# Weight chunks asked for in another order, and the w_r groups of batch 1's first half moved into batch 0, in a three-stage transformer kernel on one core

## The chip, the cores and the metric

The kernel runs on one core of a Trainium2 chip. The metric is the device time of one execution in microseconds (us). The engines are TensorE (PE; its weight loads are shown as PEld), VectorE (DVE), ScalarE (ACT), GpSimd (POOL) and SyncE (SP). DMA requests here are issued on SyncE's and ScalarE's queues, and each queue works in order.

## The reference

Inputs are float32, but the products w_r, w_k and w_v arrive as 8-byte words (the raw tiles are int32 pairs) that the kernel converts itself. Eight batches of 576 tokens, 8 heads of 64:

```python
kv  = einsum('bhsd,bhse->bhde', k, v)          # per head, 64 x 64
out = einsum('bhsd,bhde->bhse', q, kv)
x   = out / sqrt(mean(out*out, -1) + 1e-6) * g_norm   # heads side by side: 512 columns
xp  = x shifted by one token
k2  = relu((mu_k*x + (1-mu_k)*xp) @ w_k) ** 2   # 512 -> 1024
v2  = k2 @ w_v                                  # 1024 -> 512
r   = sigmoid((mu_r*x + (1-mu_r)*xp) @ w_r)     # 512 -> 512
x2  = r * v2
# then a mixture of 4 experts, each a causal attention (two chosen per token); not touched by the change
```

## The kernel before

The program has two phases. Phase 1 makes x2 and writes it to memory, phase 2 (line 600 on) reads it and computes the experts. The change is in phase 1.

Every large product is done in three passes: both factors are split into a high part (rounded for the fast fp32 mode) and a low part, and `mm3` (L62 to L64) multiplies high by high, high by low and low by high into one accumulator. A batch is handled in two halves of 288 tokens. The steps are:

- `front(b)`: kv of all heads (L229, copied by ScalarE at L233), then for each half and pair of heads the product with q (L251), its square and its copy to xT (L256, L257), the mean of squares (L269), and the reciprocal root on VectorE (`rsqrt`, L276 to L291, 14 instructions, called "root" here; result rb). `scaled` spreads rb over the heads (TensorE, L299) and multiplies xT by it (VectorE, L302). For batch 0 each half has a root of its own, first and second root; the other batches have one.
- `mix(b, h, "r")` and `mix(b, h, "k")`: the token shift (xm, L354 and L355), its high part xh (L356) and its low part xl (L346 for batch 0's r mix, L348 else), for four blocks of 128 columns.
- `r_group` (four per half, w_r, sigmoid at L374), `k_group` (eight per half, w_k, L385 to L389), `v_group` (four per half, w_v, L401). Each is a chain of `mm3` into one of four accumulators named acc.

The weights come in 20 chunks of 512 KB: 4 of w_r, 8 of w_k, 8 of w_v, in this order. `wload` asks for a chunk on ScalarE's queue (L138, tile raw, three buffers). Its conversion begins with an Abs on ScalarE (L190, tile cvt), goes on with five steps on VectorE (L146, L148, L150, L155, L157) and a copy of the high part on ScalarE (L152), and ends with three matmuls that add up the low part (L183 to L185) and a copy (L186); for four chunks VectorE does the end (L179, L180). `wstep` issues one VectorE step, `wconv` finishes one chunk and opens the next; `wstep` stands between the steps of the root, and a table `TK` says after which pieces of batch 0's front a `wconv` stands. k, v and q are loaded on SyncE's queue. A DMA signals through one of eight semaphores that both queues share in turn, so that a request waits in its queue for the eighth DMA ahead of it, and holds what stands behind it there.

The order in which the code issues work is written by hand (generators that are advanced between groups). A scheduler then settles the order on each engine from what it takes to be ready; tiles of a pool wait for a free buffer.

Of the kernel before, what the change touches and what calls it, by code (L numbers as in the profile page):

```python
# [8 lines left out]
F32 = mybir.dt.float32  # L9
# [15 lines left out]
def tile_kernel(ctx: ExitStack, tc: tile.TileContext, qT, k, v, g2, mu_k, mu_r, w_r, w_k, w_v, w_qk, w_vg, w_o, out):  # L25
    nc = tc.nc
    P = 128
# [79 lines left out]
    def phase1():  # L107
        with ExitStack() as st1:
# [22 lines left out]

            VEC = (13, 15, 17, 19)

            def wload(i):
                if i < len(wts):
                    _, _, w, kt, c0 = wts[i]
                    raw = raws[i] = stg.tile([P, CW, 2], I32, name="raw", bufs=3)
                    nc.scalar.dma_start(raw.rearrange("p n t -> p (n t)"), w[kt * P:(kt + 1) * P, c0:c0 + CW].bitcast(I32))  # L138

            def words(i):  # L140
# [26 lines left out]
            def wconv():  # L167

                i = wat[0]
                wat[0] += 1  # L170
                if 0 < i <= len(wts):
                    for _ in ops.pop():
                        pass
                    wh, wl, _, kt, c0 = wts[i - 1]
                    x = cvs.pop(i - 1)
                    raws.pop(i - 1)
                    h, l = wh[:, kt, c0:c0 + CW], wl[:, kt, c0:c0 + CW]
                    if i - 1 in VEC:
                        nc.vector.tensor_sub(x, x, h.bitcast(F32))  # L179
                        nc.vector.tensor_add(l, x, l.bitcast(F32))  # L180
                    else:
                        acc = ps.tile([P, CW], F32, name="acc", bufs=4)
                        nc.tensor.matmul(acc, ident, x, start=True, stop=False)  # L183
                        nc.tensor.matmul(acc, idn, h, start=False, stop=False)
                        nc.tensor.matmul(acc, idn, l, start=False, stop=True)  # L185
                        nc.scalar.activation(l, acc, AF.Copy)  # L186
                    wload(i + 2)
                if i < len(wts):
                    t = cvs[i] = stg.tile([P, CW], F32, name="cvt", bufs=3)
                    nc.scalar.activation(t, raws[i][:, :, 1].bitcast(F32), AF.Abs)  # L190
                    ops.append(words(i))

# [24 lines left out]
            def front(b):  # L217
# [51 lines left out]
                                nc.tensor.matmul(sm[g:g + 32, :QS], sels[:, i, :], sqs[h, i // 2][:, i % 2, c * QS:(c + 1) * QS],  # L269
                                                 start=(i == 0), stop=(i == NP - 1), skip_group_check=True)  # L270

                def rsqrt(h0, h1):
                    g = slice(64 * h0, 64 * h1)
                    m, r, t, c = ms[g], y[g], nt[g], rb[g]

# [28 lines left out]
                if b == 0:  # L304

                    for h in range(2):
                        for a in range(2):
                            heads(h, a)
                            yield
                        means(h)  # L310
                        rsqrt(h, h + 1)
                        yield
                        scaled(h)
                        yield
                    return
                for h in range(2):
                    for a in range(2):
                        heads(h, a)
                    for _ in range(3):
                        yield  # L320
                means(0, 1)
                yield
                rsqrt(0, 2)
                for _ in range(5):
                    yield
                for h in range(2):
                    scaled(h)
# [37 lines left out]

            def r_group(b, h, m):
                if m == 0:
                    sgs[b, h] = sb.tile([P, KD, HS], F32, name="sg", bufs=2)
                sg = sgs[b, h]
                xh, xl = mixed[b, h, "r"]  # L370
                acc = ps.tile([P, HS], F32, name="acc", bufs=4)
                ms_ = slice(m * P, (m + 1) * P)
                mm3(acc, lambda i: wrh[:, i, ms_], lambda i: wrl[:, i, ms_], lambda i: xh[:, i, :], lambda i: xl[:, i, :], KD)
                nc.scalar.activation(sg[:, m, :], acc, AF.Sigmoid)  # L374
# [36 lines left out]
            sk = sb.tile([P, NP, S + 1], F32, name="xT").rearrange("p k t -> p (k t)")  # L411

            sk2 = [sb.tile([P, KF, HS], F32, name=name, bufs=1).rearrange("p k t -> p (k t)") for name in ("kh", "kl")]
            sq_ = sb.tile([P, KD, HS], F32, name="sg", bufs=2)
            for c in "w0 w1 w2 k0 k1 k2 k3 k4 q0 q1 q2 q3".split():
                i = int(c[1])
                if c[0] == "w":
                    wload(i)
                elif c[0] == "k":
                    load_kv(i, [sk[:, j * DM:(j + 1) * DM] for j in (2 * i - 6, 2 * i - 5)] if i > 2 else None)  # L420
                else:
                    load_q(i, sq_[:, :2, :] if i > 2 else None)
            for i in (3, 4):
                load_kv(NF + i, [t[:, (i - 3) * DM:(i - 2) * DM] for t in sk2])
            nc.sync.dma_start(g_sb, g2)
            nc.sync.dma_start(muk, mu_k)
            nc.sync.dma_start(mur, mu_r)
# [22 lines left out]
                for _ in range(n):  # L450
                    wconv()

            TK = [1, 0, 1, 1, 0, 1, 1, 1, 1, 1, 1]
            wconv()
            for i in range(7):
                run(f0)
                ticks(TK[i])
            mr = mix(0, 0, "r")
            for i in range(4):
# [16 lines left out]
            for b in range(B):  # L476
# [7 lines left out]
                for h in range(2):  # L484
                    nb, nh = (b, 1) if h == 0 else (b + 1, 0)
                    if b == B - 1 and h == 0:
                        stf.close()
                        weights2()
                    if b > 0:
                        for m in range(1, KD):  # L490
                            r_group(b, h, m)
                            run(f)
                    mr = mix(nb, nh, "r") if 0 < nb < B else None
                    for m in range(KF):
                        k_group(b, h, m)
                        run(f)
                        if b == h == 0:
                            wconv()
                        if m > 0:
                            run(mr)  # L500
                    if mr is not None:

# [374 lines left out]
```

## Time and profile before

| | us |
|---|---|
| median of 3 runs | 1022.28 |
| lowest and highest of them | 1021.43 and 1023.65 |
| profiled execution | 1020.85 |
| its span | 1018.8 |
| TensorE busy in the span | 987.1 (97%) |
| VectorE, ScalarE, GpSimd busy | 546.8, 500.2, 248.5 |

TensorE is busy for 97% of the span, and in the page's slices its first one shows 6 tenths and the next 7 and 8, all others 9 or more. The granted clock (PEclk) is 9 or 10 tenths in every slice but the second and third, 7 and 8 tenths. A row of a timeline gives the start, the length, the engine, the line, and in brackets how long the engine was idle before it and what ended that.

### The profile page before, as it was taken

The numbers are of one execution on the slowest core, as the hardware profiler recorded it, in microseconds if no ns is written. First come the engines' busy times: TensorE is split into PE (matmuls) and PEld (weight loads), VectorE is DVE, ScalarE is ACT, GpSimd is POOL, SyncE is SP. The second block draws the span as 40 slices with busy tenths as digits, with TensorE's granted clock in tenths as the row PEclk, the third lists the DMA queues.
The fourth block names the chain that finished last, engine by engine and source line by source line (L and its number), as shares of the span: only waits on it lengthen the run. The fifth ranks groups of instructions, "written<-read, shape, count | busy, mean of one in ns | idle before, by whom it ended". The sixth has DMA issues, their size and how long they took to land.

```text
span 1018.8 us, 21026 instructions
## 1 busy us (share of the span) xinstructions
PE 987.1 (97%) x8168; PEld 899.7 (88%) x8168; DVE 546.8 (54%) x1572; ACT 500.2 (49%) x1326; POOL 248.5 (24%) x408
## 2 busy tenths in 40 slices
PE   6789999999999999999999999999999999999998
PEld 3358999999999999999999999988989898888986
DVE  4889625535535535445355531476575655656552
ACT  4677426434533553463364533456463645464544
POOL 0001212102201210220131113265161625334321
PEclk9789999999999999999999999999999999999999
DMA  9572213041050050050002201211120202020102
GB/s 324 171 231 64 67 60 106 24 112 53 25 151 27 10 164 24 1 165 24 24 2 71 60 5 43 69 48 31 65 71 24 94 1 94 18 77 27 48 12 82
DMA packets 42034, 70.56 MB, mean 69 GB/s; under 512 B 3792, under 2 KB 21712, under 8 KB 41936
## 3 DMA queue, kind: packets, MB, share of 16 engines
q1 hardware_dynamic: 30608, 49.31, 15.4%
q10 hardware_dynamic: 11328, 19.93, 6.3%
q8 instruction: 64, 1.05, 0.5%
q14 instruction: 34, 0.28, 0.1%
HBM read 50.34 MB, written 18.87 MB: 68 GB/s over the span
## 4 chain that ended last, share of the span: by engine, by line
PE 80%; DMA 7%; ACT 4%; POOL 3%; DVE 3%; issue 1%; ACTq 0%; SPq 0%; DVEq 0%; POOLq 0%
PE acc L62 22%; PE acc L64 21%; PE acc L63 21%; PE acc L725 3%; PE pt L698 3%; DMA x2in<-x2d 3%; PE s L649 2%; PE po L251 2%; POOL pr L678 2%; POOL x2l L535 2%; ACT pr L661 2%; PE acc L229 1%; PE acc L269 1%; ACT x2h L534 1%; PE po L299 1%
## 5 line engine op out<-in xcount | busy, mean ns | idle before, releaser
L388 POOL TENSOR_TENSOR ksq<-rl 128x288 f32<-128x288 f32 x128 | 92.8, 727 | 502.8 <-ACT rl L385 475.8
L62 PE MATMUL acc<-xh,wkh 128*128 128x288 f32 x512 | 153.2, 299 | 0.0
L64 PE MATMUL acc<-xh,wkl 128*128 128x288 f32 x512 | 151.6, 296 | 0.0
L64 PE MATMUL acc<-kh,wvl 128*128 128x288 f32 x512 | 151.1, 296 | 0.0
L62 PE MATMUL acc<-kh,wvh 128*128 128x288 f32 x512 | 149.4, 297 | 0.5 <-ACT kh L386 0.4
L63 PE MATMUL acc<-kl,wvh 128*128 128x288 f32 x512 | 149.6, 293 | 0.2 <-DVE kl L389 0.2
L63 PE MATMUL acc<-xl,wkh 128*128 128x288 f32 x512 | 149.4, 292 | 0.0
L661 ACT ACTIVATE pr<-pr,nm 128x256 f32<-128x256 f32 (+4 forms) x144 | 83.2, 580 | 66.5 <-DVE nm L615 65.6
L389 DVE TENSOR_TENSOR kl<-ksq,kh 128x288 fp32r<-128x288 f32 x128 | 64.4, 507 | 72.3 <-POOL ksq L388 70.6
L62 PEld LDWEIGHTS acc<-xh,wkh 128*128 128x128 f32 x512 | 96.2, 188 | 7.1 <-issue 5.3
L678 POOL TENSOR_SCALAR pr<-pr,rc,wg 128x512 f32<-128x512 f32 (+3 forms) x128 | 76.6, 613 | 99.3 <-DVE wg L608 53.9
L63 PEld LDWEIGHTS acc<-kl,wvh 128*128 128x128 f32 x512 | 97.3, 190 | 0.7 <-DVE kl L389 0.4
L63 PEld LDWEIGHTS acc<-xl,wkh 128*128 128x128 f32 x512 | 97.4, 190 | 0.1
L62 PEld LDWEIGHTS acc<-kh,wvh 128*128 128x128 f32 x512 | 95.3, 188 | 1.4 <-ACT kh L386 0.9
L64 PEld LDWEIGHTS acc<-kh,wvl 128*128 128x128 f32 x512 | 96.1, 188 | 0.0
L64 PEld LDWEIGHTS acc<-xh,wkl 128*128 128x128 f32 x512 | 96.0, 188 | 0.0
L374 ACT ACTIVATE sg<-acc 128x288 f32<-128x288 f32 x64 | 25.9, 408 | 142.6 <-PE acc L64 142.6
L348 DVE TENSOR_TENSOR xl<-xm,xh 128x288 fp32r<-128x288 f32 x120 | 54.4, 487 | 75.9 <-ACT xh L356 75.3
L401 DVE TENSOR_TENSOR sg<-acc,sg 128x288 f32<-128x288 f32 x64 | 29.2, 457 | 105.9 <-PE acc L64 105.1
L385 ACT ACTIVATE rl<-acc 128x288 f32<-128x288 f32 x128 | 52.1, 414 | 58.7 <-PE acc L64 58.3
L62 PE MATMUL acc<-x2h,wqh 128*128 128x256 f32 (+1 forms) x256 | 78.6, 308 | 0.0
L62 PE MATMUL acc<-xh,wrh 128*128 128x288 f32 x256 | 77.1, 302 | 1.1 <-ACT wvl L186 1.1
(166 smaller groups left out, 2437.3 us busy)
## 6 DMA issues: line engine op xcount, KB each, us to landing
x2d<-sg SPq DMA_DIRECT2D x16, 576.0 KB, 3.3
qt<-in_qT SPq DMA_DIRECT2D x31, 288.0 KB, 4.8
out<-ob SPq DMA_DIRECT2D x28, 288.0 KB, 2.1
kt<-in_k SPq DMA_DIRECT2D x24, 256.0 KB, 5.2
vt<-in_v SPq DMA_DIRECT2D x24, 256.0 KB, 5.7
x2in<-x2d ACTq DMA_DIRECT2D x8, 640.0 KB, 4.4
raw<-in_w_k ACTq DMA_DIRECT2D x8, 512.0 KB, 4.5
raw<-in_w_v ACTq DMA_DIRECT2D x8, 512.0 KB, 3.5
```

The lines of the kernel that those rows point to most:

```text
L62: nc.tensor.matmul(ps, wh(i), xh(i), start=(i == 0), stop=False)
L63: nc.tensor.matmul(ps, wh(i), xl(i), start=False, stop=False)
L64: nc.tensor.matmul(ps, wl(i), xh(i), start=False, stop=(i == n - 1))
L348: nc.vector.tensor_sub(xl[:, p, :], xp, xh[:, p, :].bitcast(F32))
L385: nc.scalar.activation(rl, acc, AF.Relu)
L388: nc.gpsimd.tensor_mul(sq, rl, rl)
L389: late.append(lambda: nc.vector.tensor_sub(kl[:, m, :], sq, kh[:, m, :].bitcast(F32)))
L401: nc.vector.tensor_mul(sg[:, m, :], acc, sg[:, m, :])
L661: nc.scalar.activation(pr[:, :L], pr[:, :L], AF.Exp, bias=nm, scale=-1.0, accum_out=sms[b, p, j][:, e2:e2 + 1])
L678: nc.gpsimd.tensor_scalar(pr[:, :L], pr[:, :L], rc[:, r:r + 1], wg, op0=ALU.mult, op1=ALU.mult)
L698: nc.tensor.transpose(pt[:, (i - i0) * P:(i - i0 + 1) * P], pr[:, k1 - P:k1], ident)
L725: nc.tensor.matmul(y[r * D:(r + 1) * D, a:w], vs[:, i, e * D:(e + 1) * D], pT[:, r, i, a:w], start=(i == 0), stop=(i == idx[-1]), skip_gro ...
```

## The change

The first weight requests and the first k and v requests come in another order: five chunks are asked for before anything is converted, the fourth and fifth into tiles that are still free (those of the mix, xh and xl). Each later chunk is then asked for two conversions earlier in the first part. cvt has two buffers instead of three, sg three instead of two. The first root is called with an empty step in place of `wstep`, and TK has one tick more. The loads of batch 1's last pieces of k and v into kh and kl move from the beginning to behind the third piece of the front. In batch 1's front fewer empty steps are taken, its r mix is made amid the k groups of batch 0's first half, and its four r groups stand behind the fifth of these k groups. They stood behind the k groups of batch 0's second half (the first of them) and at the start of batch 1 (the other three).

```diff
--- before.py
+++ after.py
@@ -131,10 +131,12 @@
 
             VEC = (13, 15, 17, 19)
 
-            def wload(i):
+            def wload(i, raw=None):
                 if i < len(wts):
                     _, _, w, kt, c0 = wts[i]
-                    raw = raws[i] = stg.tile([P, CW, 2], I32, name="raw", bufs=3)
+                    if raw is None:
+                        raw = stg.tile([P, CW, 2], I32, name="raw", bufs=3)
+                    raws[i] = raw
                     nc.scalar.dma_start(raw.rearrange("p n t -> p (n t)"), w[kt * P:(kt + 1) * P, c0:c0 + CW].bitcast(I32))
 
             def words(i):
@@ -184,9 +186,13 @@
                         nc.tensor.matmul(acc, idn, h, start=False, stop=False)
                         nc.tensor.matmul(acc, idn, l, start=False, stop=True)
                         nc.scalar.activation(l, acc, AF.Copy)
-                    wload(i + 2)
+
+                    if i - 1 < 3:
+                        wload(i + 4)
+                    elif i - 1 > 4:
+                        wload(i + 2)
                 if i < len(wts):
-                    t = cvs[i] = stg.tile([P, CW], F32, name="cvt", bufs=3)
+                    t = cvs[i] = stg.tile([P, CW], F32, name="cvt", bufs=2)
                     nc.scalar.activation(t, raws[i][:, :, 1].bitcast(F32), AF.Abs)
                     ops.append(words(i))
 
@@ -269,7 +275,7 @@
                                 nc.tensor.matmul(sm[g:g + 32, :QS], sels[:, i, :], sqs[h, i // 2][:, i % 2, c * QS:(c + 1) * QS],
                                                  start=(i == 0), stop=(i == NP - 1), skip_group_check=True)
 
-                def rsqrt(h0, h1):
+                def rsqrt(h0, h1, wstep=wstep):
                     g = slice(64 * h0, 64 * h1)
                     m, r, t, c = ms[g], y[g], nt[g], rb[g]
 
@@ -308,7 +314,7 @@
                             heads(h, a)
                             yield
                         means(h)
-                        rsqrt(h, h + 1)
+                        rsqrt(h, h + 1, *([lambda: None] if h == 0 else []))
                         yield
                         scaled(h)
                         yield
@@ -316,12 +322,12 @@
                 for h in range(2):
                     for a in range(2):
                         heads(h, a)
-                    for _ in range(3):
+                    for _ in range(1 if b == 1 else 3):
                         yield
                 means(0, 1)
                 yield
                 rsqrt(0, 2)
-                for _ in range(5):
+                for _ in range(2 if b == 1 else 5):
                     yield
                 for h in range(2):
                     scaled(h)
@@ -365,7 +371,7 @@
 
             def r_group(b, h, m):
                 if m == 0:
-                    sgs[b, h] = sb.tile([P, KD, HS], F32, name="sg", bufs=2)
+                    sgs[b, h] = sb.tile([P, KD, HS], F32, name="sg", bufs=3)
                 sg = sgs[b, h]
                 xh, xl = mixed[b, h, "r"]
                 acc = ps.tile([P, HS], F32, name="acc", bufs=4)
@@ -411,17 +417,16 @@
             sk = sb.tile([P, NP, S + 1], F32, name="xT").rearrange("p k t -> p (k t)")
 
             sk2 = [sb.tile([P, KF, HS], F32, name=name, bufs=1).rearrange("p k t -> p (k t)") for name in ("kh", "kl")]
-            sq_ = sb.tile([P, KD, HS], F32, name="sg", bufs=2)
-            for c in "w0 w1 w2 k0 k1 k2 k3 k4 q0 q1 q2 q3".split():
+            sq_ = sb.tile([P, KD, HS], F32, name="sg", bufs=3)
+            sw = [sb.tile([P, KD, HS], F32R, name=name, bufs=2).rearrange("p k t -> p (k t)")[:, :2 * CW].bitcast(I32).rearrange("p (n t) -> p n t", t=2) for name in ("xh", "xl")]
+            for c in "w0 w1 k0 k1 w2 k2 k3 w3 k4 q0 q1 w4 q2 q3".split():
                 i = int(c[1])
                 if c[0] == "w":
-                    wload(i)
+                    wload(i, sw[i - 3] if i > 2 else None)
                 elif c[0] == "k":
                     load_kv(i, [sk[:, j * DM:(j + 1) * DM] for j in (2 * i - 6, 2 * i - 5)] if i > 2 else None)
                 else:
                     load_q(i, sq_[:, :2, :] if i > 2 else None)
-            for i in (3, 4):
-                load_kv(NF + i, [t[:, (i - 3) * DM:(i - 2) * DM] for t in sk2])
             nc.sync.dma_start(g_sb, g2)
             nc.sync.dma_start(muk, mu_k)
             nc.sync.dma_start(mur, mu_r)
@@ -450,10 +455,13 @@
                 for _ in range(n):
                     wconv()
 
-            TK = [1, 0, 1, 1, 0, 1, 1, 1, 1, 1, 1]
+            TK = [1, 1, 1, 1, 0, 1, 1, 1, 1, 1, 1]
             wconv()
             for i in range(7):
                 run(f0)
+                if i == 2:
+                    for c in (3, 4):
+                        load_kv(NF + c, [t[:, (c - 3) * DM:(c - 2) * DM] for t in sk2])
                 ticks(TK[i])
             mr = mix(0, 0, "r")
             for i in range(4):
@@ -486,17 +494,27 @@
                     if b == B - 1 and h == 0:
                         stf.close()
                         weights2()
-                    if b > 0:
+                    if b > 0 and (b, h) != (1, 0):
                         for m in range(1, KD):
                             r_group(b, h, m)
                             run(f)
-                    mr = mix(nb, nh, "r") if 0 < nb < B else None
+                    mr = mix(nb, nh, "r") if 0 < nb < B and (nb, nh) != (1, 0) else None
                     for m in range(KF):
                         k_group(b, h, m)
                         run(f)
                         if b == h == 0:
                             wconv()
-                        if m > 0:
+                            if m == 0:
+                                mr = mix(1, 0, "r")
+                            run(mr)
+                            if m == KD:
+
+                                for m2 in range(KD):
+                                    r_group(1, 0, m2)
+                                    run(f)
+                                    wconv()
+                                mr = None
+                        elif m > 0:
                             run(mr)
                     if mr is not None:
```

ScalarE's queue at the start of the program, before (names are tile or input; DMAHW0 to DMAHW7 are the eight DMA semaphores):

```order
L138 DMA raw<-in_w_r 128x1024 x3
L444 ACT_TABLE_LOAD
L444 ACTIVATE idn<-ident 128x128 [waits Pool_49]
L190 ACTIVATE cvt<-raw 128x512 [waits DMAHW0_49]
L190 ACTIVATE cvt<-raw 128x512 [waits DMAHW3_49]
L152 ACTIVATE wrh<-cvt 128x512 [waits DVE_49]
L138 DMA raw<-in_w_r 128x1024 [waits DMAHW0_49,DVE_49]
L190 ACTIVATE cvt<-raw 128x512 [waits DMAHW5_49]
```

The same place with the change:

```order
L140 DMA raw<-in_w_r 128x1024 x3
L140 DMA xh<-in_w_r 128x1024
L140 DMA xl<-in_w_k 128x1024 [waits DMAHW1_49]
L449 ACT_TABLE_LOAD
L449 ACTIVATE idn<-ident 128x128 [waits Pool_49]
L196 ACTIVATE cvt<-raw 128x512 [waits DMAHW0_49]
L196 ACTIVATE cvt<-raw 128x512 [waits DMAHW3_49]
L154 ACTIVATE wrh<-cvt 128x512 [waits DVE_49] x2
L140 DMA raw<-in_w_k 128x1024 [waits DMAHW4_49,DVE_49]
L196 ACTIVATE cvt<-raw 128x512 [waits DMAHW5_49,PE_49,Activation_49]
L140 DMA raw<-in_w_k 128x1024 [waits DMAHW7_49,DVE_49]
```

Two more requests stand ahead of the table load, the second behind a wait, and the next two (the sixth and seventh chunk) stand around the third Abs.

VectorE at the first root, before (ms, nt and y are the root's tiles, cvt and raw those of a conversion):

```order
L276 TENSOR_SCALAR ms<-acc 64x144
L278 TENSOR_SCALAR nt<-ms 64x144
L280 TENSOR_SCALAR y<-nt 64x144
L283 TENSOR_TENSOR nt<-y 64x144
L429 TENSOR_SCALAR nuk<-muk 128x4
L429 TENSOR_SCALAR nur<-mur 128x4
L285 TENSOR_TENSOR nt<-nt,ms 64x144
L287 SCALAR_TENSOR_TENSOR y<-nt,y 64x144
L146 TENSOR_SCALAR cvt<-cvt 128x512
L283 TENSOR_TENSOR nt<-y 64x144
```

and with the change:

```order
L282 TENSOR_SCALAR ms<-acc 64x144
L150 TENSOR_SCALAR cvt<-cvt 128x512
L159 SCALAR_TENSOR_TENSOR wkl<-raw 128x512
L284 TENSOR_SCALAR nt<-ms 64x144
L152 SCALAR_TENSOR_TENSOR cvt<-raw,cvt 128x512
L286 TENSOR_SCALAR y<-nt 64x144
L157 TENSOR_SCALAR raw<-cvt 128x512
L289 TENSOR_TENSOR nt<-y 64x144
L159 SCALAR_TENSOR_TENSOR wkl<-raw 128x512
L291 TENSOR_TENSOR nt<-nt,ms 64x144
```

Conversion steps lie between the root's steps in both; with the change they begin at its first step.

TensorE at the scaling matmuls of batch 1, before (kh, kl and wvh, wvl are the factors of batch 0's v groups):

```order
L62 MATMUL acc<-kh,wvh 128x288
L63 MATMUL acc<-kl,wvh 128x288
L64 MATMUL acc<-kh,wvl 128x288
L299 MATMUL po<-rb,selb 128x144 x8
L63 MATMUL acc<-kl,wvh 128x288
L64 MATMUL acc<-kh,wvl 128x288
```

and with the change, where wkh and wkl are the factors of the fifth k group of batch 0's first half and wrh and wrl those of batch 1's r groups:

```order
L62 MATMUL acc<-xh,wkh 128x288
L63 MATMUL acc<-xl,wkh 128x288
L64 MATMUL acc<-xh,wkl 128x288
L305 MATMUL po<-rb,selb 128x144 x16
L62 MATMUL acc<-xh,wrh 128x288 x4
L63 MATMUL acc<-xl,wrh 128x288
L64 MATMUL acc<-xh,wrl 128x288
```

The 16 scaling matmuls stand in one piece, and the first matmuls of four r groups, one for each accumulator, right behind them.

## Rows read from the trace of the kernel before

**Rows 1.** Windows, from:to in us, length, each engine's busy us, PEclk, DMA share, GB/s

```profile
25.00:30.00 5.00, 1.61 (x5) 0.68 (x4) 3.75 (x15) 2.14 (x4) 0.00 (x0) 1.00 1.03 337
90.00:140.00 50.00, 50.00 (x375) 48.65 (x374) 35.80 (x81) 25.47 (x60) 13.07 (x17) 1.00 0.15 45
```

**Rows 2.** Waits of TensorE, 0 to 130 us: total us, times, longest

```profile
PE acc L229 <- DMA vt<-in_v: 6.5, 1, 6.5
PE acc L183 <- DVE cvt L150: 4.6, 3, 3.4
PE po L251 <- ACT kv L233: 2.7, 1, 2.7
PE po L299 <- DVE rb L291: 2.0, 1, 2.0
```

**Rows 3.** Waits of VectorE, 0 to 130 us: total us, times, longest

```profile
DVE cvt L146 <- ACT cvt L190: 15.2, 8, 6.4
```

**Rows 4.** Timeline of ScalarE at the start: start, us, operation, idle before and its releaser

```profile
2.14 1.28 ACT L444 ACT_TABLE_LOAD   x1 [2.14 <-issue]
3.44 0.31 ACT L444 ACTIVATE idn<-ident 128x128 fp32r<-128x128 f32 x1
4.85 0.66 ACT L190 ACTIVATE cvt<-raw 128x512 f32<-128x512 f32 x1 [1.10 <-DMA raw<-in_w_r]
...
11.40 0.68 ACT L190 ACTIVATE cvt<-raw 128x512 f32<-128x512 f32 x1 [3.15 <-DMA vt<-in_v]
...
20.36 0.38 ACT L233 ACTIVATE kv<-acc 128x256 f32<-128x256 f32 x1 [3.42 <-DMA kl<-in_v]
...
21.68 0.65 ACT L256 ACTIVATE sq<-po 128x576 f32<-128x576 f32 x1
22.21 0.66 ACT L257 ACTIVATE xT<-po 128x576 f32<-128x576 f32 x1
```

**Rows 5.** DMA issues, 0 to 60 us: count, KB, us to landing

```profile
muk<-in_mu_k SPq DMA_DIRECT2D x1, 2.0 KB, 6.5
```

**Rows 6.** Timeline of VectorE, first and second root

```profile
21.82 0.43 DVE L146 TENSOR_SCALAR cvt<-cvt 128x512 f32<-128x512 f32 x1 [6.44 <-ACT cvt L190]
...
24.77 0.30 DVE L276 TENSOR_SCALAR ms<-acc 64x144 f32<-64x144 f32 x1
...
33.62 0.35 DVE L291 SCALAR_TENSOR_TENSOR rb<-rb,lom,y 64x144 fp32r<-64x144 f32 x1
...
44.26 0.31 DVE L276 TENSOR_SCALAR ms<-acc 64x144 f32<-64x144 f32 x1 [1.22 <-PE acc L269]
...
59.64 0.37 DVE L291 SCALAR_TENSOR_TENSOR rb<-rb,lom,y 64x144 fp32r<-64x144 f32 x1
```

**Rows 7.** Timeline of VectorE, root of batch 1 and its mix

```profile
107.62 0.37 DVE L291 SCALAR_TENSOR_TENSOR rb<-rb,lom,y 128x144 fp32r<-128x144 f32 x1
...
109.20 1.79 DVE L302 SCALAR_TENSOR_TENSOR xT<-xT,g_sb,po 128x288 f32<-128x288 f32 x4 [0.84 <-PE po L299]
...
117.39 0.45 DVE L348 TENSOR_TENSOR xl<-xm,xh 128x288 fp32r<-128x288 f32 x1
```

**Rows 8.** Timeline of TensorE, batch-1 loads, fifth k group, scaling matmuls

```profile
53.76 0.22 PE L229 MATMUL acc<-kl,kh 112*64 112x64 f32 x1
...
99.23 0.30 PE L64 MATMUL acc<-xh,wkl 128*128 128x288 f32 x1
99.36 0.29 PE L62 MATMUL acc<-xh,wkh 128*128 128x288 f32 x1
...
108.71 0.67 PE L299 MATMUL po<-rb,selb 32*128 32x144 f32 x8
...
112.69 0.44 PE L299 MATMUL po<-rb,selb 32*128 32x144 f32 x4
```

**Rows 9.** Windows, VectorE alone, from the second root on

```profile
60.00:108.00 48.00, 43.90 (x96) 0.93 0.38 119
```

**Rows 10.** Windows, the slow stretch behind the second root

```profile
62.50:69.40 6.90, 5.96 (x22) 3.20 (x19) 5.68 (x13) 6.90 (x16) 0.00 (x0) 0.52 0.73 217
```

## The prediction

> **What bounds the kernel now.** I read the windows first. From 25 to 30 us TensorE is busy 1.61 of 5.00 us; from 90 to 140 us it is busy 50.00 of 50.00 at a granted clock of 1.00 [rows 1]. So the kernel has a start of some 62 us with holes and a long saturated part. A change that moves matmuls inside the saturated part earns nothing by itself; only the holes of the start and the slow-clock stretches can be won, and any new hole in the saturated part is paid in full. The waits of TensorE name the holes: 6.5 us on the loads of v, 4.6 us (three waits) on conversion steps of VectorE, 2.7 us on the copy of kv, 2.0 us on the second root's end [rows 2]. Together that is 15.8 us, all before 62 us. VectorE for its part waits 15.2 us, in eight places, for the Abs that opens a conversion [rows 3]. Then I read the order of both programs for what stands where, and the timelines for the prices.
>
> **Part 1, the loads.** Five chunks are asked for first; the two new requests stand on ScalarE's queue ahead of its activation-table load (order of ScalarE in the section on the change). The fifth request waits for a semaphore that the first load of k frees. That load and the chunk w0 are asked for together; the first Abs, which waited for w0, began at 4.85 [rows 4], so I take 5.2 for k. Behind it come the request (0.34), the table load (1.28) and idn (0.31): first Abs at about 7.1 instead of 4.85, +2.3. The next three requests wait for loads asked for earlier: the sixth chunk's for the fourth load of v, ahead of the third Abs. With 1.05 MB of w3 and w4 now ahead of or beside k, v and q at the 337 GB/s that the rows show for a stretch in which the DMA engines are all busy (share 1.03) [rows 1], what is displaced comes up to 1.05/0.337 = 3.1 us later. The third Abs, at 11.40 before [rows 4], comes at about 15.0. The eighth chunk's request waits for the load of muk, one of the last of the first round; it took 6.5 us from issue to landing [rows 5], which puts it near 20.6. Behind that request ScalarE has four operations of about 0.5 us pitch ahead of the kv copy, so kv is written at about 23.0 instead of 20.36 [rows 4]: +2.6.
>
> The Trainium skill ("Trainium Kernel Development and Optimization", section Key Constraints) says that loads issued from several engines' queues run on the same 16 DMA engines and interleave, so that more queues save issue time only. By that rule the early w3 and w4 buy no bandwidth, only an order; the windows with share 1.03 agree.
>
> **Part 2, the first root.** In the code its steps stand without conversion steps between. In the built order ten conversion steps still lie among its 14 (before: eleven); the scheduler puts them where they are ready. I therefore give this part nothing. The root begins when kv's products are squared and summed and the conversion steps ahead of it are through: behind kv, at 23.0, stand eight ScalarE operations at a pitch of 0.53 [rows 4], the Abs of the seventh chunk last, so that this Abs ends near 27.9; two conversion steps at 0.43 follow on VectorE: first root at 28.8, against 24.77. It lasted 9.2 us from the start of L276 to the end of L291, 24.77 to 33.97 [rows 6]; with one step fewer and without its inner wait it may be a little shorter, and I take the same: 38.0. From there to the second root were 10.3 us and 16 instructions; now there are 17, one more at 0.45: 48.75. The second root took 15.75 us for 35 instructions, 0.45 each [rows 6]. It now has 25, since ten conversion steps have been done earlier: 25 x 0.45 = 11.25, end at 60.0. Before it ended at 60.01. Call that end X. The delay of the start and the shorter second root cancel: term 0.0. Its bounds: if kv is held no longer than before, X is 2.6 earlier; if the loads of the first round land 3.1 later as a whole, X is 3 later. So -3 to +3, and 0 because both chains are made from rows.
>
> After X the conversion is one chunk further on, so TensorE and VectorE have the same work to do as before or a little less. The 1.1 us wait of the r groups for a converted chunk stays or goes; I count it as staying.
>
> **Part 3, the r groups of batch 1.** Before, the scaling matmuls (L299) of batch 1 stand amid the v groups of batch 0 and the chain behind them is covered by those. The root's result rb began at 107.62 and was there at 107.99; the last xl of the r mix at 117.39 to 117.84 [rows 7], 9.85 us later, under a TensorE that had other matmuls. Now 16 scaling matmuls and all 48 r matmuls stand in one piece behind the fifth k group, and all four accumulators belong to them, so nothing else can run in the meantime (second order fence).
>
> When does TensorE come there? Its order from X to the end of the fifth k group is the same work. Before, that group's last matmul began just ahead of 99.36, so X + 39.3 [rows 8]. When is rb there? VectorE has 76 instructions between X and rb; before, it had 94 in 48.0 us (60.01 to 107.99), 0.51 each: 38.8. So rb and TensorE arrive together at X + 39. From rb to the last xl VectorE has 25 instructions, six of them conversion and kl steps that come before the scaling. Between 109.20 and 117.39 it began 20 instructions, 0.41 each, and four of L302 took 1.79, 0.45 each [rows 7]; at 0.43 the 25 take 10.8 us, near the 9.85 that the shorter list of before took. The last contraction step of the four groups, 12 matmuls at 0.133 (start to start, [rows 8]), follows: X + 38.8 + 10.8 + 1.6 = X + 51.2. Without a wait TensorE would be through at X + 39.3 + 1.6 (scaling matmuls, 0.67 for eight and 0.44 for four [rows 8], twice the four) + 6.4 (48 x 0.133) = X + 47.3. New wait: 3.9 us. Its bounds: VectorE was busy 43.90 us for 96 instructions [rows 9], 0.457 each; if it never waits, rb is at X + 34.8 and the wait is nothing; if rb is as late against TensorE as 4 us the other way, 8. I take 3.9, since 0.51 is what the same stretch measured with its waits. It is all on the path: every later matmul moves by it.
>
> **The clock.** The hole of 2.0 us ahead of the second root's scaling, at 60.06, and smaller ones behind it, were followed by a stretch from 62.5 to 69.4 with a granted clock of 0.52, TensorE busy 5.96 of 6.90 us [rows 2, 10]; at 1.2 instead of 2.4 GHz some half of that is lost, up to 3.45. A hole of 3.9 us is longer than any of these, but stands behind 40 us without one. I put half of 3.45 for such a stretch behind it: 1.7, bounds 0 and 3.45.
>
> The Trainium skill ("TensorE: Matmul & The Clock Gate", section Why this matters for your kernels) advises against idle gaps between bursts of matmuls, since the clock then falls. By it the slow stretch would come in full (3.45, sum 7.3); by the rows it may, as a hole amid saturated work is not shown.
>
> **What costs nothing.** The loads of batch 1 moved behind the third step of the front: first used at 53.76 by TensorE [rows 8], some 30 us after they can be asked for; if they came late, the wait of rows 2 on v would show again. Two cvt buffers instead of three: an Abs now waits for the chunk before last, which is through when VectorE is the limit. A third sg buffer, and fewer empty steps in front(1): order only. The r groups no longer at the end of batch 0 and start of batch 1: TensorE saturated both ways.
>
> **Sum.** 0.0 + 3.9 + 1.7 = 5.6 us on the profiled execution's 1020.85 (span 1018.8 and 2.05 around it): 1026.45. The median shown, 1022.28, lies 1.43 above that execution, so 1027.9; I say 1028.
>
> **Rivals.** (a) The start shrinks. With five chunks in flight VectorE's longest wait, 6.44 us ahead of 21.82 [rows 6], goes; conversions are done while kv is still loading; both roots end some 5 us earlier, and the slow stretch of 3.45 at 62.5 with it, as its holes go. The r wait stays at 3.9: 1022.28 - 5 - 3.45 + 3.9 = 1017.7, and 1013.8 if VectorE, one chunk ahead, has rb early. For it: TensorE's holes are all in the start, and the second root is ten steps shorter. Against it: the third Abs and kv stand behind requests that wait. It decides if kv is written before about 20.5. (b) Start and r wait cancel: X 3 earlier, wait 3.9, no slow stretch: 1023; or rb 4 us early and X unmoved: 1022. (c) Everything late: X +3, wait 8, slow stretch 3.45: 14 us, 1036; half-way, 1033. That the change does not do what it says holds for the first root alone, and its price of nothing is in the sum.
>
> **Chances.** My forecast 0.50, its own range 1024.5 to 1032; (a) 0.26; (b) 0.14; (c) 0.10. About 0.2%, 2 us, is what a measurement of this kernel can tell from no change. Faster: 0.26; same: 0.14; slower: 0.60. The range leaves out the lower part of (a) and the upper half of (c): 1016 to 1034.
>
> **What would show it.** Right: the first Abs near 7 us and kv near 23; the second root's end near 60; a wait of TensorE on xl or xT at L62 or L305 of 3 to 5 us at about 105, with a granted clock below 1 behind it; after 120 us the same stages, all shifted by a constant. Wrong: kv before 20.5 and a second root that ends before 57, or a TensorE without a hole behind the fifth k group.

## The result, and the profile after

| | before | changed |
|---|---|---|
| median of 4 runs, us | 1021.86 | 1033.13 |
| lowest and highest | 1020.43, 1023.65 | 1030.95, 1035.76 |
| profiled execution and its span | 1020.85, 1018.8 | 1033.03, 1031.0 |

The ratio is 1.0116 (95% interval 1.0096 to 1.0136): the change costs some 12 us. The forecast's sign held, and so did the whole range, 1016 to 1034. The time is 5 us above the forecast of 1028 and outside its own range, 1024.5 to 1032; it lies where rival (c), everything late, had its half-way point, 1033. The change is twice the 5.6 us of the sum.

How much of it is there by when? The stores of x2 on SyncE's queue, one for each half of a batch, are milestones. That of batch 2's first half, before (start, length, queue, line):

```profile
257.27 0.53 SPq L403 DMA_DIRECT2D x2d<-sg  x1
```

and changed:

```profile
267.17 0.53 SPq L409 DMA_DIRECT2D x2d<-sg  x1
```

So 9.9 us are lost before this store, and the distance stays at 9.9 (to 0.03 us) up to the store of batch 6's first half (544.01 before, 553.94 changed); it is 10.7 at the next one and 12.2 in the span. Most of the loss is made early, and the rows say where. First ScalarE at the start, changed (answers to [rows 4]):

```profile
4.92 1.28 ACT L449 ACT_TABLE_LOAD   x1 [4.92 <-DMA kt<-in_k]
...
6.42 1.41 ACT L196 ACTIVATE cvt<-raw 128x512 f32<-128x512 f32 x2
...
16.15 0.66 ACT L196 ACTIVATE cvt<-raw 128x512 f32<-128x512 f32 x1 [5.29 <-DMA xT<-in_k]
...
21.56 0.33 ACTq L140 DMA_DIRECT2D raw<-in_w_k  x1
...
24.62 0.38 ACT L239 ACTIVATE kv<-acc 128x256 f32<-128x256 f32 x1 [0.53 <-PE acc L235]
```

The table load waited for the first load of k, the first Abs came at 6.42 (forecast 7.1), the third at 16.15 (15.0), behind a request that waited 5.29 us, and kv at 24.62 (23.0) behind another one. VectorE's timeline, changed (answers to [rows 6 and 7]), at both roots, at a conversion's last operation, at the root of batch 1 and at the last xl of its r mix:

```profile
30.93 0.29 DVE L282 TENSOR_SCALAR ms<-acc 64x144 f32<-64x144 f32 x1
...
38.83 0.36 DVE L297 SCALAR_TENSOR_TENSOR rb<-rb,lom,y 64x144 fp32r<-64x144 f32 x1
...
50.97 0.31 DVE L282 TENSOR_SCALAR ms<-acc 64x144 f32<-64x144 f32 x1
...
61.28 0.37 DVE L297 SCALAR_TENSOR_TENSOR rb<-rb,lom,y 64x144 fp32r<-64x144 f32 x1
...
86.58 0.68 DVE L182 TENSOR_TENSOR wvl<-cvt,wvl 128x512 fp32r<-128x512 f32 x1
...
99.69 0.77 DVE L297 SCALAR_TENSOR_TENSOR rb<-rb,lom,y 128x144 fp32r<-128x144 f32 x1
...
111.66 0.44 DVE L354 TENSOR_TENSOR xl<-xm,xh 128x288 fp32r<-128x288 f32 x1
```

The first root began at 30.93 (forecast 28.8), the second ended at 61.65 (60.0; before 60.01): 1.64 us late. From there to batch 1's rb it is 38.8 us, as forecast. TensorE, changed (answers to [rows 8]):

```profile
88.01 1.10 PE L185 MATMUL acc<-cvt,ident 128*128 128x512 f32 x2 [2.06 <-ACT cvt L196]
...
101.88 0.67 PE L305 MATMUL po<-rb,selb 32*128 32x144 f32 x8
105.28 0.44 PE L305 MATMUL po<-rb,selb 32*128 32x144 f32 x4 [2.73 <-DVE xT L308]
106.13 0.65 PE L305 MATMUL po<-rb,selb 32*128 32x144 f32 x4 [0.41 <-DVE xT L308]
107.31 1.33 PE L62 MATMUL acc<-xh,wrh 128*128 128x288 f32 x4 [0.53 <-ACT xh L362]
109.76 0.61 PE L63 MATMUL acc<-xl,wrh 128*128 128x288 f32 x1 [1.12 <-DVE xl L354]
```

and where the sixth k group begins:

```profile
117.16 0.29 PE L62 MATMUL acc<-xh,wkh 128*128 128x288 f32 x1
```

From the second root's end to the scaling matmuls it is 40.2 us, 0.9 more than before; in it lies a wait of 2.06 us for an Abs. What that Abs waited for stands in ScalarE's timeline:

```profile
87.30 0.67 ACT L196 ACTIVATE cvt<-raw 128x512 f32<-128x512 f32 x1 [0.90 <-DVE wvl L182]
```

It waited for L182, which ended at 87.26 (86.58 above): the last reader of the cvt buffer that the Abs writes. Behind this wait of TensorE the clock was low for a while:

```profile
88.00:92.50 4.50, 4.49 (x18) 0.63 0.39 130
```

At a granted clock of 0.63 another 1.7 us of the 4.49 are lost, so wait and clock together take 3.7. That the stretch is only 0.9 longer than before has two reasons: the slow stretch behind the second root was milder (62.50 to 69.40, clock 0.75 and 4.42 us busy, before 0.52 and 5.96 [rows 10]), and the kernel before lost 1.11 us ahead of 85.78, waiting for wvl. Then the hole: from 101.88 to 117.16, 15.3 us for 16 scaling and 48 r matmuls that take 8.0 without waits (1.6 and 6.4). Its waits are 2.73, 0.41, 0.53 and 1.12, in sum 4.8. The rest, 2.5, is the clock. The windows, changed, first the one that answers to [rows 1], then the hole's second part:

```profile
90.00:140.00 50.00, 45.22 (x311) 43.61 (x311) 32.87 (x74) 24.86 (x59) 8.09 (x11) 0.91 0.14 45
```

```profile
106.40:113.00 6.60, 4.95 (x21) 4.40 (x20) 6.00 (x15) 3.57 (x8) 0.00 (x0) 0.50 0.42 128
```

TensorE was busy 4.95 us at a granted clock of 0.50 from 106.4 to 113, amid the last waits and behind them, which loses half of 4.95. Sum: 1.64 + 0.9 + 7.3 = 9.8 of the 9.9. The waits as the waits view names them (total, times, longest):

```profile
PE po L305 <- DVE xT L308: 3.1, 2, 2.7
...
PE acc L185 <- ACT cvt L196: 2.1, 1, 2.1
PE acc L63 <- DVE xl L354: 1.1, 1, 1.1
```

### The profile page after: what moved, and what is told of

It is laid out like the page before. It is cut to its first block, busy times and chain, and to the rows that moved or that the text cites. A ratio compares the mean times of both kernels' runs of the same rounds, so it can differ in the third digit from the quotient of the medians.

```text
span 1031.0 us, 21025 instructions
## 1 busy us (share of the span) xinstructions
PE 990.1 (96%) x8168; PEld 903.7 (88%) x8168; DVE 543.7 (53%) x1572; ACT 502.6 (49%) x1326; POOL 246.6 (24%) x408
## 4 chain that ended last, share of the span: by engine, by line
PE 79%; DMA 6%; DVE 5%; ACT 5%; POOL 3%; issue 1%; ACTq 0%; SPq 0%; DVEq 0%; POOLq 0%
PE acc L62 22%; PE acc L64 21%; PE acc L63 21%; PE pt L716 3%; PE acc L743 3%; PE s L667 2%; DMA x2in<-x2d 2%; ACT pr L679 2%; POOL x2l L553 2%; PE po L257 2%; PE acc L235 1%; POOL pr L696 1%; PE s L652 1%; ACT x2h L552 1%; DMA raw<-in_w_k 1%
```

## The experiments

Each run's median stands beside that of the kernel before on the same chip. "Part 3" is the r groups of batch 1 with all that goes with them.

**Part 3 undone**, all else as changed: the old conditions at the r groups and the mix, the old empty steps, two sg buffers.

```diff
-                    if b > 0 and (b, h) != (1, 0):
+                    if b > 0:
-                            if m == KD:
-                                for m2 in range(KD):
-                                    r_group(1, 0, m2)
...
```

> The changed kernel with part 3 undone: batch 1's r groups, its r mix, the empty steps of its front and the sg buffers as before; loads, cvt buffers, ticks and first root as changed. Theory (the wait behind the fifth k group is the main loss): the hole and the slow clock behind it, together 7.3 us in the changed kernel's profile, go; what stays is the later second root, 1.6 us, and up to 1 us behind it: 1023.5 to 1025.5. Rival (the new order of the loads is the main loss): 1029 or more.

Measured 1026.54 beside 1020.61, ratio 1.0060 (1.0044 to 1.0077). The hole's part of the loss is gone, but 1 us more is left than the upper end of what was expected: the rest of the change has a price too, 6 us.

**Part 3 alone** on the kernel before.

```diff
-t = cvs[i] = stg.tile([P, CW], F32, name="cvt", bufs=3)
+t = cvs[i] = stg.tile([P, CW], F32, name="cvt", bufs=2)
... (and the lines of part 3)
```

> The kernel before with part 3 alone (r groups of batch 1 behind the fifth k group, sg with three buffers), and cvt with two buffers, without which the third sg buffer does not fit. Theory: the full price of the hole, 7 to 9 us: 1029 to 1031. Rival (loads): 1022 to 1024.

Measured 1034.28 beside 1020.61, ratio 1.0133 (1.0113 to 1.0153): 13.7 us, more than the whole change. Neither theory had that. Part 3 alone and the rest alone add up to 19.6, both at once cost 11.3: something is counted twice, and what the two kernels share is the cvt buffers.

**Loads, cvt buffers and tick alone**; differs from the first run by the first root.

```diff
-                        rsqrt(h, h + 1, *([lambda: None] if h == 0 else []))
+                        rsqrt(h, h + 1)
```

> The kernel before with the loads, the cvt buffers and the tick as changed, but the first root with its conversion steps called between, and part 3 undone. It differs from the first kernel of this set by the first root alone. If the empty steps of the first root cost or gain nothing, as the prediction had it: within 1 us of that kernel. If they do what their words say: 2 us or more apart.

Measured 1024.74 beside 1020.61 (1.0042, 1.0026 to 1.0057); the first run lies 1.8 above, with overlapping runs (1023.49 to 1025.91 and 1024.48 to 1028.93); in the traces the store of batch 2's first half is 0.5 apart (259.51 and 260.05). Inconclusive by the bound of 1 us, and the next run is the better test.

**The first root alone** on the kernel before.

```diff
-                        rsqrt(h, h + 1)
+                        rsqrt(h, h + 1, *([lambda: None] if h == 0 else []))
```

> The kernel before with the first root's empty steps alone. Prediction: no price, 1021 to 1023. If the root comes out in one piece and ends some 5 us earlier: 1017 to 1019; if conversions fall behind by its ten steps: 1025 or more.

Measured 1020.40 beside 1020.61, ratio 0.9995 (0.9983 to 1.0007): nothing, as forecast.

**The r groups two k groups later.**

```diff
-                            if m == KD:
+                            if m == KF - 2:
```

> The changed kernel, with batch 1's four r groups behind the seventh k group instead of the fifth. TensorE then comes 3.2 us of k work later and the scaling matmuls lie amid k groups. Theory (wait of 4.8 us plus its slow clock): at most 1.6 us of wait and no or little slow clock are left; the median falls by 5 to 7 us to 1026 to 1028. Rival (the place does not matter, moving them at all costs): unchanged within 1.5 us of 1033.

Measured 1029.57 beside 1020.58 (1.0088, 1.0072 to 1.0104): 9.0 more than the kernel before, where the changed one is 11.3 more, so 2.3 less and not 5 to 7. The place matters, but 3.2 us of k work did not buy 3.2 us of wait. TensorE's timeline of this run shows what is left:

```profile
105.71 0.45 PE L305 MATMUL po<-rb,selb 32*128 32x144 f32 x4 [0.43 <-DVE xT L308]
106.93 0.44 PE L305 MATMUL po<-rb,selb 32*128 32x144 f32 x4 [0.78 <-DVE xT L308]
108.01 1.33 PE L62 MATMUL acc<-xh,wrh 128*128 128x288 f32 x4 [0.64 <-ACT xh L362]
110.39 0.61 PE L63 MATMUL acc<-xl,wrh 128*128 128x288 f32 x1 [1.05 <-DVE xl L354]
```

The four waits are 2.9 us where they were 4.8, and the clock fell again (0.57 from 106.9 to 114.6, with 5.98 us busy: 2.6 lost), so the hole takes 5.5 instead of 7.3. The chain itself moved: the last scaling matmuls and the first xl came later than in the changed kernel (106.93 and 110.39 against 106.13 and 109.76).

**The r groups behind the v groups of batch 0's first half.**

```diff
-                            if m == KD:
-                                for m2 in range(KD):
...
                     run(mk)
+                    if b == h == 0:
+                        for m2 in range(KD):
+                            r_group(1, 0, m2)
+                            run(f)
+                            wconv()
```

> The changed kernel, with the four r groups behind the four v groups of batch 0's first half: 24 us of k and v work lie between the scaling matmuls' earliest start and the first r matmul. Theory: no wait and no slow clock there, 7 to 8 us less than the changed kernel: 1025 to 1026.5, as with part 3 undone (1026.5). Rival: a cost of part 3 besides its wait would leave it above 1028.

Measured 1025.94 beside 1020.58 (1.0053, 1.0035 to 1.0071), and TensorE's window there:

```profile
100.00:130.00 30.00, 30.00 (x229) 1.00 0.18 57
```

30.00 of 30.00 busy at a clock of 1.00. The third sg buffer, the fewer empty steps and the earlier mix are all still in this kernel, and it stands within 1 us of the one with part 3 undone: to that 1 us, the hole is the whole price of part 3.

**Part 3 undone, three cvt buffers**, and **two cvt buffers alone** on the kernel before: one line each, in opposite directions.

```diff
-t = cvs[i] = stg.tile([P, CW], F32, name="cvt", bufs=2)
+t = cvs[i] = stg.tile([P, CW], F32, name="cvt", bufs=3)
```

> Part 3 undone, as in the first run, and cvt back at three buffers (there is room with two sg buffers). If the 2.48 us wait of TensorE for a conversion at 86.9 us in that run comes from the second buffer missing, it goes: 1 to 4 us faster than 1026.5. If it comes from VectorE's amount of work: the same within 1 us.

> The kernel before with two cvt buffers instead of three. Prediction: no price, within 1.5 us of before (1020.6). If two buffers hold back the Abs of the next chunk: a new wait of TensorE on a conversion between 80 and 100 us and 2 us or more slower.

Three buffers: 1023.12 beside 1020.58 (1.0019, 1.0007 to 1.0030), 3.4 less than with two. Two buffers alone: 1027.38 beside 1020.58 (1.0062, 1.0046 to 1.0077), 6.8 us for one number. TensorE in the latter, at the first matmul of a conversion, and an Abs on ScalarE:

```profile
82.29 1.28 PE L183 MATMUL acc<-cvt,ident 128*128 128x512 f32 x2 [1.91 <-DVE cvt L150]
...
98.28 1.10 PE L183 MATMUL acc<-cvt,ident 128*128 128x512 f32 x2 [3.30 <-DVE cvt L150]
```

```profile
99.47 0.68 ACT L190 ACTIVATE cvt<-raw 128x512 f32<-128x512 f32 x1 [0.67 <-PE acc L183]
```

Neither wait of TensorE is in [rows 2], whose three waits of this kind are all before 62 us. So the third cvt buffer was at work: with two, an Abs stands behind the last reader of the chunk before last, on VectorE (L182 in the changed kernel, 87.30) or on TensorE (here the L183 of 98.28, which stands amid k groups).

The traces, one execution each, put the same three steps at the store of batch 2's first half: 267.17 with the whole change, 260.05 with part 3 undone, 256.55 with three cvt buffers besides, 257.27 before. So the hole takes 7.1, the missing buffer 3.5, and what is left, the loads, the tick and the first root, costs nothing before this store (0.7 the other way). How far one execution can be trusted, the second root's end tells: it lies at 61.06 to 63.07 in the four kernels that have the changed start and two cvt buffers (changed, part 3 undone, r groups at either other place).

Where then are the 2.5 us by which the kernel with three buffers is slower than before? In its trace the distance is -0.7 up to batch 6's first half and 1.9 at the next store. Between the two, TensorE waits for kh at the v groups of batch 6's second half:

```profile
566.22 0.40 PE L62 MATMUL acc<-kh,wvh 128*128 128x288 f32 x1 [1.23 <-ACT kh L392]
```

With another 0.40 behind it, and a clock of 0.83 (565 to 575, with 8.23 us busy; before 1.00 and 9.38), that makes the 2.6. The kernel before waits 0.40 for kh at this place, the changed one 0.85 and 0.40.

**Requests on GpSimd's queue.** To see what ScalarE loses by requests that wait, the kernel before with the fourth to eighth chunk's (then all later ones) requested from GpSimd:

```diff
-                    nc.scalar.dma_start(
+                    (nc.gpsimd if 3 <= i < 8 else nc.scalar).dma_start(
```

> The kernel before, with the requests of the fourth to eighth chunk on GpSimd's queue instead of ScalarE's, so that no request that waits stands ahead of ScalarE's work in the first 25 us. Theory (requests in ScalarE's queue hold the Abs and the kv copy behind them): third Abs near 9 instead of 11.4, kv near 17 to 18 instead of 20.4, second root's end 2 to 3 us earlier, median 2 to 3 us lower: 1017 to 1019. Rival (VectorE's conversions or the landing of the chunks set the start): kv earlier, but second root's end and median as before within 1 us.

(`99` in place of `8` in the second.)

> As the run before it in this set, with all requests from the fourth chunk on on GpSimd's queue, also those beside the later front. Theory: as that run or up to 1 us faster; the requests behind 30 us held little (waits of ScalarE on loads of w_v: 2.2 us).

Measured 1025.75 (1.0044, 1.0030 to 1.0058) and 1024.22 (1.0031, 1.0018 to 1.0043) beside 1021.29: slower by 4.5 and 2.9. The first lies outside what theory and rival had, the second 1.5 below the first, where up to 1 was expected. ScalarE was freed as expected, in the first of them:

```profile
9.02 0.67 ACT L190 ACTIVATE cvt<-raw 128x512 f32<-128x512 f32 x1 [0.75 <-DMA raw<-in_w_r]
...
17.20 0.38 ACT L233 ACTIVATE kv<-acc 128x256 f32<-128x256 f32 x1
...
19.49 0.67 ACT L190 ACTIVATE cvt<-raw 128x512 f32<-128x512 f32 x1
```

The third Abs came at 9.02 and kv at 17.20. But the fourth chunk's Abs came only at 19.49, and VectorE waited for it and for muk:

```profile
20.19 0.43 DVE L146 TENSOR_SCALAR cvt<-cvt 128x512 f32<-128x512 f32 x1 [6.90 <-ACT cvt L190]
...
25.07 0.17 DVE L429 TENSOR_SCALAR nuk<-muk 128x4 f32<-128x4 f32 x1 [3.98 <-DMA muk<-in_mu_k]
```

With 6.90 and 3.98 us of waiting on VectorE, its first root began at 25.75, later than before (24.77). The second ended at 59.43 all the same, 0.6 earlier than before; the loss comes up on TensorE later, behind a wait for a conversion (with a clock of 0.74 from 95 to 100):

```profile
93.66 1.51 PE L183 MATMUL acc<-cvt,ident 128*128 128x512 f32 x2 [2.31 <-DVE cvt L150]
```

The profiled execution of the second, 1021.96, is one of its fastest, and up to the store of batch 2's first half it shows no loss (256.31). Of the theory the part on ScalarE holds; what it leaves out, as I read it, is that VectorE needs chunks to convert in the time that ScalarE gains, and falls behind later without them. The five early chunks are such chunks, and so the same edit on the kernel with part 3 undone and three cvt buffers, from the sixth chunk on:

```diff
-                    nc.scalar.dma_start(
+                    (nc.gpsimd if 5 <= i < 99 else nc.scalar).dma_start(
```

> The changed kernel's loads and first root, part 3 undone, three cvt buffers (the run with 1023.1), with all requests from the sixth chunk on on GpSimd's queue. Theory: what is left of part 1's price, 2 to 2.5 us, is ScalarE's work held behind these requests; third Abs near 11 to 12 instead of 15.5 to 16, kv at 19 to 21 instead of 24 to 25, median 1019 to 1021. Rival (w3 and w4 take the DMA engines' time ahead of k, v and q): kv and median stay within 1 us.

Measured 1016.37 beside 1021.29, ratio 0.9953 (0.9940 to 0.9967): faster than before, by 4.9. ScalarE and VectorE in this run:

```profile
9.36 0.66 ACT L196 ACTIVATE cvt<-raw 128x512 f32<-128x512 f32 x1
...
11.07 0.69 ACT L196 ACTIVATE cvt<-xh 128x512 f32<-128x512 f32 x1 [0.34 <-PE acc L185]
...
18.68 0.38 ACT L239 ACTIVATE kv<-acc 128x256 f32<-128x256 f32 x1
```

```profile
25.22 0.17 DVE L434 TENSOR_SCALAR nuk<-muk 128x4 f32<-128x4 f32 x1 [6.46 <-DMA muk<-in_mu_k]
...
27.48 0.29 DVE L282 TENSOR_SCALAR ms<-acc 64x144 f32<-64x144 f32 x1
```

With three cvt buffers the third Abs was at 9.48 already, ahead of the request that waits; what the other queue wins is the fourth Abs, 11.07 instead of 16.03 (there after 5.18 us of idling behind that request), and kv, 18.68 instead of 24.30. The second root ends at 58.15 instead of 61.63. VectorE had converted five chunks by 18.8 and then waited 6.46 us for muk, only to compute nuk. The last run gives nuk and nur to GpSimd:

```diff
-                nc.vector.tensor_scalar(nu, mu, -1.0, 1.0, op0=ALU.mult, op1=ALU.add)
+                nc.gpsimd.tensor_scalar(nu, mu, -1.0, 1.0, op0=ALU.mult, op1=ALU.add)
```

> The fastest version so far (changed loads and first root, part 3 undone, three cvt buffers, requests from the sixth chunk on on GpSimd's queue), with the two small operations nuk and nur on GpSimd instead of VectorE, which waited 6.46 us for muk there at 18.8 to 25.2 us. Theory (VectorE is the limit of the start): the conversion of the sixth chunk begins at 22.6, the first root at about 24.9 instead of 27.48, the second ends 2 to 2.6 us earlier than 58.15, median 1013.5 to 1015. Rival (the next chunks' landing or the clock takes it back): first root earlier, median within 1 us of 1016.4.

Measured 1014.16 beside 1020.12, ratio 0.9939 (0.9920 to 0.9958). Both roots, and the window of [rows 1]:

```profile
24.81 0.29 DVE L282 TENSOR_SCALAR ms<-acc 64x144 f32<-64x144 f32 x1
...
56.09 0.37 DVE L297 SCALAR_TENSOR_TENSOR rb<-rb,lom,y 64x144 fp32r<-64x144 f32 x1
```

```profile
90.00:140.00 50.00, 50.00 (x382) 49.28 (x381) 28.60 (x65) 20.89 (x49) 10.42 (x14) 1.00 0.11 35
```

The second root ends at 56.46, 3.6 us ahead of the kernel before. It beats both kernels: 6.0 us under the one before, and some 17 under the changed one, each taken beside its own kernel before. Against the run ahead of it the last step is not clear of noise in the medians (the intervals overlap); in the traces the store of batch 2's first half comes 2.1 earlier.

## Why the prediction was right in sign and half in size

- **Part 1, the loads.** The chain was read rightly (request ahead of the table load, requests ahead of the third Abs and of kv). The first Abs came 0.7 us earlier than worked out, the other places 1 to 2 us later. The start's term was 0.0 within -3 to 3; the second root's end measured +1.64, and at the store of batch 2's first half the trace with three cvt buffers shows no price. That kernel's 1.9 us over the one before (by its ratio; 2.5 between the medians) come, in its trace, behind batch 6's first half. The third Abs was held by the two cvt buffers too: with three it came at 9.48, the request being as late.
- **Part 2, the first root.** Right: no price, since the built order keeps conversion steps amid the root.
- **Part 3, the hole.** Right in place and kind. Wait 3.9, measured 4.8; clock 1.7, measured 2.5; sum 5.6, measured 7.3 in the trace. Between medians it is 6.9 (part 3 alone less two cvt buffers alone) and, by the ratios of the changed kernel and of the one with part 3 undone, 1.0116 and 1.0060, 5.7. That the wait came out near is in part luck: it was reckoned by the last xl, for which TensorE did not wait. It ended at 112.10, and TensorE waited for nothing from 109.76 to 117.16; 3.1 of the 4.8 us were waits for xT in the scaling matmuls, ahead of that.
- **The step that failed** is "Two cvt buffers instead of three: an Abs now waits for the chunk before last, which is through when VectorE is the limit", costed at nothing. It costs 3.4 us between the medians with part 3 undone and 6.8 alone; in the changed kernel's trace wait and clock take 3.7. The chunk before last is not through: its last reader stands behind other work on TensorE or on VectorE. [Rows 3] already had VectorE waiting 15.2 us for the Abs; with two buffers alone it is 17.4, and the sum should have had a term for it.
- **All stages shifted by a constant after 120 us:** not so. The shift is 9.9 us up to batch 6's first half and 12.2 at the end, 2.3 for which the sum had no term.
- **The sum by runs:** 5.34 (hole) + 3.39 (cvt) + 2.54 (the rest) = 11.27, all between medians. These are steps of one row of kernels, from the changed one back to the one before, so that their sum has to come out; only the single terms say something.
- **Rival (a), a start that shrinks,** was a real possibility of these loads. With the requests off ScalarE's queue and three buffers kv is at 18.68 and the kernel 4.9 us faster. But kv before about 20.5 does not decide it alone, as the prediction had it: on the kernel before, with kv at 17.20, the same move cost 4.5 us.

Three things stay open. Behind batch 6's first half the changed kernel loses another 2.3 us, of which 0.8 comes before the next store, with the longer waits for kh; other kernels here lose up to 2.9 before that store (the one with r groups behind the v groups, in the slowest of its six executions), and no run shows what makes kh late. Why VectorE's chain moved later in the run with the r groups two k groups later was not tried. And why moving the requests slows the kernel before is argued from one trace.

## What to carry to other kernels

A buffer given up to pay for another is a change of its own: look up who waits for its readers, and time it alone. A DMA request that must wait holds the compute engine in whose queue it stands, so early loads belong where nothing else waits, and in these runs they paid only where the engines had chunks to convert in the time won. Work with a long chain ahead of it goes where other matmuls cover that chain.

## What was not expected of the hardware

Waits can cost twice: those of 0.41, 0.53, 1.12 and 2.73 us within 8 us came with 6.6 us at 0.50 of the clock, although TensorE had been at 1.00 just ahead of them (95 to 102); the run with 2.9 us of such waits lost the clock as well. But the clock does not follow the waits alone. The wait of 2.06 us ahead of 88.01 lost it in the changed kernel, and the same wait at the same line did not with the r groups two k groups later:

```profile
88.53 1.10 PE L185 MATMUL acc<-cvt,ident 128*128 128x512 f32 x2 [2.06 <-ACT cvt L196]
```

```profile
88.00:93.00 5.00, 4.47 (x28) 1.00 0.45 161
```

Nor did a single wait of 3.30 us before 98.28 (two cvt buffers alone):

```profile
98.00:104.00 6.00, 5.72 (x37) 1.00 0.00 0
```

So neither the sum of the waits nor the longest one tells it in these runs, and what does is not shown. The Trainium skill ("TensorE: Matmul & The Clock Gate", section Why this matters for your kernels), by which the prediction would have put the slow stretch in full, agrees with the first case and not with the last.

A request on GpSimd's queue took 0.53 to 1.42 us of GpSimd each, and the chunks of w_k took 7.1 us from issue to landing (the median, in the run with 1016.37), against 4.7 on ScalarE's queue (in the run with 1023.12). The Trainium skill ("DMA: Bandwidth & Descriptors", section Issuing engines are not separate DMA queues) says that issuing from several engines only saves the sequencer's time to initiate a DMA, which is usually small. In these two runs moving requests to another queue was worth some 7 us between the medians (1023.12 beside 1020.58 became 1016.37 beside 1021.29). 3.8 us of it are there at the store of batch 2's first half (256.55 and 252.73), and not by faster loads: what went is the wait that such a request makes ScalarE's work share, 5.18 us ahead of the fourth Abs. The rest lies behind batch 6's first half, and no run ties it to the requests.
